# Attention tiles at the other end of SBUF, closed early; w_sp's norms, scale and block sums planned into the first stage's z2; plain units removed

## The chip, the cores and the metric

The kernel runs on one core of one Trainium2 chip. A core has five engines that run their own instruction streams: PE (TensorE, matrix products into eight PSUM banks of 128 x 512 f32), DVE (VectorE), ACT (ScalarE), POOL (GpSimd) and SP (SyncE, which here only issues DMAs). SBUF is the on-chip memory of 128 partitions. The metric is the device time of one execution in microseconds (us). Before the change three runs gave 1127.93, 1130.12 and 1130.16 us; the median is 1130.12 us.

## What is computed

Two layers, each an attention block and a gated MLP block, on x of 2048 x 576, in bfloat16. The attention looks at 8 positions at distance 2 and has 32 heads of 18. The MLP block mixes along the sequence with the 2048 x 2048 matrix w_sp:

```python
def _B_ref(x, w_in, w_sp, b_sp, w_out):
    z = _gelu(jnp.einsum('bsd,df->bsf', x, w_in))
    z1 = z[..., :Fh].copy()
    z2 = _layernorm(z[..., Fh:], axis=-1)
    g = jnp.einsum('ts,bsf->btf', w_sp, z2) + b_sp[None, :, None]
    return jnp.einsum('bsf,fd->bsd', z1 * g, w_out)

x = x + _A_ref(_layernorm(x, axis=-1), A_wqkv, A_wo)
x = x + _B_ref(_layernorm(x, axis=-1), B_w_in, B_w_sp, B_b_sp, B_w_out)
x = x + _A_ref(_layernorm(x, axis=-1), A_wqkv, A_wo)
x = x + _B_ref(_layernorm(x, axis=-1), B_w_in, B_w_sp, B_b_sp, B_w_out)
```

Both layers use the same weights. Fh is 2304.

## The kernel before

Five stages run one after the other: phase_F(0), phase_S(1), phase_F(2), phase_S(3), phase_E.

**phase_F** is an attention stage with z2 at its end. It describes its work as steps (name, engine, estimated cost, key, function, steps that must come before, buffers taken) and hands them to a planner, the class Flow. The planner simulates the engines with the estimated costs. It repeatedly takes the engine that can start something earliest, and on it, of the steps that can start at that time, the one with the lowest key (line 191). The order in which it takes the steps is the order in which instructions are issued, so each engine's stream is fixed when the kernel is built. A step that takes "H" needs a pair of PSUM banks, one that takes "PT" a single bank. The attention steps carry keys near the number of their tile (0 to 17), z2's steps the key KZ + KS * i with KZ = 169.61 and KS = 25.3 in the first layer (line 1056), for i from 0 to 15.

z2 of row tile i (Z2_steps, line 883) is three products of 128 x 768 on PE (lines 895 and 902), a gelu on ACT for each (918), a sum of squares on DVE (928) and ACT (933), eight small steps on POOL (939 to 946) and the normalisation on DVE (949). From i = 7 the products go in groups of three.

**phase_S** is the spatial stage. w_sp's rows are handled in two halves c of 1024, the upper half c = 0 first, and z in nine column blocks jj. Each (c, jj) is a unit, 18 in all, in an order written out by hand, with no planner. An ordinary unit (unit, line 1197) multiplies a 2 x 2 split of w_sp's half by z with seven block products for two column halves s: blocks A11, A12, S1, S2, S4, S3, A22, each 8 matmuls of 128 x 512 (eight, line 1181), 56 in all. S1 to S4 are sums and differences of the blocks in f16; T1 to T4 are the same kind of sums of z (t_op, line 1187), made on DVE one unit ahead. Between them stand plus (line 1205) and times_u (1195) on DVE. Each unit also makes z1 of the next one on PE (1156, 1164) with gelus on ACT (1168). The f16 blocks need w_sp multiplied by a power of two, which comes from the sum of all absolute values: norm_part (1077) sums one 128 x 2048 part on ACT or DVE, norm_sum (1085) adds up, scales (1088) totals over the partitions with a PE matmul against ones and makes scale and inverse in five small DVE steps.

In the first layer w_sp is not ready in blocks. So phase_S(1) loads the upper half with four transposing DMAs (line 1279, on SP) into A11, A12, S3's and A22's space, takes norms, and runs units 0 and 1 as plain units (line 1249): four blocks by two halves s, 64 matmuls each, on unscaled blocks in unit 0 and 1, while ACT and DVE take the norms of both halves and scale (lines 1329 to 1339) and DVE makes S1, S2, S4 and, in unit 2, S3 (1333, 1342, 1343, 1432). The lower half is made block by block in eight pieces during units 3 to 7: four transposing DMAs (piece_load), a scaling on ACT (1376), six sums on DVE (1383) and a store to DRAM on POOL's queue; the store of piece k starts the load of piece k + 2 on SP. The table at line 1350 says where in which unit each step of a piece stands. The finished blocks of the upper half are stored from line 1415 for the second layer, and unit 8 loads the lower half's blocks. phase_S(3) loads all from DRAM.

**Memory.** The tiles of phase_F, attention and others, come from one pool that closes when the phase ends. A tile of a later pool that lies over an earlier tile waits for the last use of that tile.

Of the kernel before, what the change touches and what calls it, by code (L numbers as in the profile page):

```python
# [10 lines left out]
ACT = mybir.ActivationFunctionType  # L11
# [9 lines left out]
P = 128  # L21
# [24 lines left out]
EPS = 1e-5  # L46
BLOCKS = ("A11", "A12", "A22", "S3", "S1", "S2", "S4")
# [219 lines left out]
class K:  # L267
# [17 lines left out]
    def setup(self):  # L285
# [23 lines left out]
        self.first_pairs = None  # L309
# [219 lines left out]
    def phase_F(self, li):  # L529
# [3 lines left out]
        pool = self.pool = cm.__enter__()  # L533
        x_prev = self.A_x if first else self.xres[0]
# [7 lines left out]
                  0.8 if first else 0.0, first)  # L542
        wB = pool.tile([P, 3, 2 * D], bf16, name="wB")
        zst = pool.tile([P, NS // 2, 11], f32, name="zst")
        Pb = [pool.tile([P, 4, 8, HP], bf16, name=f"P{k}") for k in range(2)]
        wo = pool.tile([P, 5, D], bf16, name="wo")
        vbi = [pool.tile([P, H * (DH + 1)], i32, name=f"v_ext{k}") for k in range(3)]
# [3 lines left out]
        oT = pool.tile([P, 5, RING], bf16, name="oT")  # L551
        o_tb = [pool.tile([P, D if first else D + HP], bf16, name=f"o_t{k}") for k in range(2)]
        oq = [self.zu[:, NB, a:a + 5 * P].rearrange("p (c n) -> p c n", n=P) for a in (0, 2176)]
        xt = {}

        def x_tile(i):
            if i < NXZ:
                return self.zu[:, NB - 1, D * i:D * (i + 1)]
            if i not in xt:
                xt[i] = pool.tile([P, D], bf16, name="xt", bufs=NX)  # L560
            return xt[i][:]
# [11 lines left out]
        QKb = [pool.tile([P, 16 * R], bf16, name=f"QK{k}") for k in range(NQK[ly])]  # L573
# [83 lines left out]
        def QK_steps(g, key):  # L657
# [16 lines left out]
            for d in range(NM):  # L674
# [6 lines left out]
                def ev(e, d=d):  # L681
                    if d % 2 == 0:
                        box["s", d // 2] = pool.tile([P, 4 * QT * max(sizes)], bf16, name="stg", bufs=NSTG[ly])
                    to = box["s", d // 2][:, 2 * gw * (d % 2):2 * gw * (d % 2 + 1)]
                    self.copy(e, to.rearrange("p (r q j) -> p q r j", q=2, r=2), box[d][:, :, 0:gw].rearrange("p q (j r) -> p q r j", r=2))
# [19 lines left out]
            def ev4(e):  # L705
                to = box[NM, "s"] = pool.tile([HP, 2 * QT * max(sizes)], bf16, name="stx", bufs=NSTX[ly])
# [51 lines left out]
        def ATT_steps(t, key):  # L758
# [42 lines left out]
            def fin(_):  # L801
                o_t = box["o"] = o_tb[t % 2][:, 0:D]
                O = box["O"][:, :, 0:16 * (DH + 1)].rearrange("p s (h e) -> p s h e", e=DH + 1)
                rec = pool.tile([P, 2, 16], f32, name="rec", bufs=2)
# [279 lines left out]

    def norm_sum(self, norms):
        self.nc.vector.tensor_reduce(out=self.wsc[:, 4:5], in_=norms, axis=AX.X, op=ALU.add)

    def scales(self, c, ones, ps):
# [3 lines left out]
        col = [wsc[:, k:k + 1] for k in range(7)]  # L1092
        bits = [k.bitcast(i32) for k in col]
        nc.tensor.matmul(ps, lhsT=ones, rhs=col[4], start=True, stop=True)
        self.pairs += 1
        nc.vector.tensor_copy(out=col[5], in_=ps)
# [5 lines left out]
    def phase_S(self, li):  # L1102
# [6 lines left out]
        low = ("S1",) if first else ("A22", "S1")  # L1109
        A = {n: pool.tile([P, 8, 512], f16 if n[0] == "S" else bf16, name=n) for n in low}  # L1110
        T = pool.tile([P, 4, 8, P], f16, name="T")
        tmp = [pool.tile([P, 512], f32, name=f"g{k}") for k in range(3)]
        A |= {n: pool.tile([P, 8, 512], f16 if n[0] == "S" else bf16, name=n) for n in ("S2", "S3", "S4", "A22", "A12", "A11") if n not in low}
# [12 lines left out]
        w1s = {}  # L1126

        def load_w1(jj, c):
            w1 = pool.tile([P, 2 * NM + 1, P], bf16, name="w1", bufs=2)
            self.load576(lambda s: w1[:, NM * s:NM * s + NM, :], w1[:, 2 * NM, :], self.B_w_in[:, P * jj:P * (jj + 1)],  # L1130
                         self.B_w_in[:, 1152 + P * jj:1152 + P * (jj + 1)], (nc.sync,))
            w1s[jj, c] = w1
# [54 lines left out]
        def t_op(jj, k):  # L1187

            B = z_of(jj)
            a, b = {1: (B[0, 1], B[0, 0]), 2: (B[1, 1], T[:, 0]), 3: (B[1, 1], B[0, 1]), 4: (B[1, 0], T[:, 1])}[k]  # L1190
            nc.vector.tensor_tensor(out=T[:, k - 1], in0=a, in1=b, op=ALU.subtract)
# [5 lines left out]
        def unit(n, jj, c, z1, t_next, at):  # L1197
# [21 lines left out]
            eight(v, T[:, 0], A["S1"], True)  # L1219
# [4 lines left out]
            eight(y, T[:, 1], A["S2"], False)  # L1224
# [7 lines left out]
            eight(y, T[:, 2], A["S3"], False)  # L1232
# [7 lines left out]
            eight(y, T[:, 3], A["A22"], False)  # L1240
# [8 lines left out]
        def plain(jj, c, banks, raw, order, after):  # L1249
            B, u = z_of(jj), u_of(jj, c)  # L1250
            met = set()
            for a, b in order:
                for s in range(2):
                    eight(self.psum[:, banks[a].start + s, :], B[b, s], raw[a, b], a not in met)
                after(a, b)
                if a in met:
                    for s in range(2):
                        g = tmp[(2 * a + s) % 3][:].bitcast(bf16)[:, 0:512]
                        nc.vector.tensor_tensor(out=g, in0=self.psum[:, banks[a].start + s, :], in1=bias(c, a), op=ALU.add)
                        times_u(u, a, s, g)  # L1260
                met.add(a)

        def load_ops(c, names):
            for nm in names:
                if c == 0:
                    self.dma(A[nm][:].rearrange("p i t -> p (i t)"), self.ops[c, nm][:])
                else:
                    to = A[nm][:].bitcast(bf16) if nm[0] == "S" else A[nm][:]
                    self.dma(to.rearrange("p i t -> p (i t)"), self.ops1[:, BLOCKS.index(nm), :])

        ORDER = ("A11", "A12", "S1", "S2", "S4", "S3", "A22")
        Wt = self.B_w_sp
        wAf = self.wA[:].rearrange("p a n -> p (a n)")
        todo = {}
        if first:
            raw = {(0, 0): A["A11"][:], (0, 1): A["A12"][:], (1, 0): A["S3"][:].bitcast(bf16), (1, 1): A["A22"][:]}
            for a in range(2):
                for b in range(2):
                    nc.sync.dma_start_transpose(out=raw[a, b], in_=Wt[512 * a:512 * a + 512, 1024 * b:1024 * b + 1024])
            load_w1(0, 0)  # L1280
            flat = {n: A[n][:].bitcast(bf16).rearrange("p i t -> p (i t)") for n in ("S1", "S2", "S4")}
            nat = [flat[n][:, 2048 * k:2048 * k + 2048] for n, k in (("S4", 0), ("S2", 0), ("S2", 1), ("S1", 0), ("S1", 1))]
            nat += [wAf[:, 2048 * k:2048 * k + 2048] for k in range(3)]

            def load_nat(k):
                self.dma(nat[k], Wt[1024 + P * k:1024 + P * k + P, :])
            for k in range(3):
                load_nat(k)
            load_w1(1, 0)
            for k in range(3, 7):  # L1290
                load_nat(k)
        else:
            load_ops(0, ("A11", "A12"))
            load_w1(0, 0)
            load_ops(0, ("S1", "S2", "S4", "S3"))
            load_w1(1, 0)
        q = nc.gpsimd if first else nc.sync
        load_b(0, 0, q)
# [230 lines left out]
```

## Time and profile before

| what | value |
|---|---|
| median of three runs | 1130.12 us |
| lowest and highest | 1127.93 and 1130.16 us |
| the profiled execution | 1131.26 us |
| its span, first to last instruction | 1129.5 us |
| mean granted TensorE clock | 0.997 |

A row of busy time by stretches gives start and end in us from the span's start, the length, then the busy us and the instruction count of each engine, the TensorE clock that was granted as a share of full speed, the busy share of the DMA engines and GB/s. A row of a timeline gives start, duration, engine, line of the kernel, operation, out<-in tiles and the number of instructions merged; in brackets stands how long the engine was idle before it and what ended that idle time. Matmuls overlap in their records, so steady progress is read from start to start. Rows of one line's instructions give min/median/max duration in ns.

### The profile page before, as it was taken

To read this page: it belongs to the slowest core of one execution; us is meant where nothing else is said; L and a number is where in the kernel's file an instruction comes from. 1 tells how busy PE (TensorE), PEld (TensorE's weight loads), DVE (VectorE), ACT (ScalarE), POOL (GpSimd) and SP (SyncE) were. 2 spreads that over 40 slices of the span, in tenths; PEclk is the share of its full clock that TensorE was granted. 3 is DMA by queue.
4 is the path that set the end of the run, shared out by engine and by line. 5 is a ranking of instruction groups with operands and counts; after the bars stand their busy time and mean duration, and the time that the engine had idled before them with its cause. 6 is when DMAs were issued, how large, how long until landed. Compare 5 with 4: busy or idle time off the path is not lost.

```text
span 1129.5 us, 24544 instructions
## 1 busy us (share of the span) xinstructions
PE 1108.1 (98%) x10163; PEld 614.6 (54%) x10163; DVE 696.5 (62%) x1152; ACT 442.1 (39%) x689; POOL 265.2 (23%) x574
## 2 busy tenths in 40 slices
PE   8899999999999999999999989999999999999998
PEld 5677655444434444447677765554444444444677
DVE  8788855687666555554566778556555555555311
ACT  7678877883232011102455678872101110111000
POOL 6244488501111000004101215882000000000000
PEclk9899999999999999999999999999999999999999
DMA  7776372345879532115344585702112283221221
GB/s 191 150 133 143 68 164 81 97 147 149 267 214 325 184 104 58 48 50 138 66 77 84 108 169 105 271 1 77 41 47 59 77 315 87 75 58 38 84 64 53
DMA packets 187304, 131.82 MB, mean 117 GB/s; under 512 B 145241, under 2 KB 171481, under 8 KB 183609
## 3 DMA queue, kind: packets, MB, share of 16 engines
q1 hardware_dynamic: 179864, 100.47, 35.0%
q0 software_dynamic: 7328, 29.79, 8.1%
q8 instruction: 79, 1.29, 0.5%
q14 instruction: 33, 0.26, 0.1%
HBM read 68.40 MB, written 31.20 MB: 88 GB/s over the span
## 4 chain that ended last, share of the span: by engine, by line
PE 65%; DVE 1%; ACT 1%; DMA 1%; issue 1%; POOL 0%; DVEq 0%; ACTq 0%; POOLq 0%
PE psum L1183 29%; PE psum L479 12%; PE psum L1156 8%; PE psum L895 6%; PE psum L389 3%; PE psum L737 2%; PE psum L863 1%; DMA S<-op 1%; PE psum L1164 1%; PE psum L902 1%; PE psum L797 1%; PE psum L775 1%; PE psum L383 0%; ACT P L782 0%; ACT v_ext L460 0%
## 5 line engine op out<-in xcount | busy, mean ns | idle before, releaser
L1168 ACT ACTIVATE zu<-psum 128x1024 bf16<-128x1024 f32 x72 | 73.2, 1022 | 396.8 <-PE psum L1164 363.8
L1205 DVE SCALAR_TENSOR_TENSOR g<-psum,wsc,bsp 128x512 f32<-128x512 f32 (+1 forms) x136 | 101.9, 750 | 141.7 <-PE psum L1183 141.5
L1183 PE MATMUL psum<-S,T 128*128 128x512 f16 x816 | 187.2, 379 | 1.0 <-DVE g L1205 0.9
L1183 PEld LDWEIGHTS <-T 128*128 128x128 f16 x1088 | 106.3, 98 | 130.0 <-issue 1.9
L1183 PEld LDWEIGHTS <-zu 128*128 128x128 bf16 x944 | 92.4, 98 | 114.7 <-issue 3.8
L1183 PE MATMUL psum<-A,zu 128*128 128x512 bf16 x640 | 144.2, 379 | 0.0
L1156 PE MATMUL psum<-xnD,w 128*128 128x512 bf16 x576 | 136.3, 380 | 0.0
L479 PEld LDWEIGHTS <-zu 128*128 128x128 bf16 x1152 | 112.3, 98 | 29.6 <-issue 0.4
L1205 DVE SCALAR_TENSOR_TENSOR g<-psum,wsc,g 128x512 bf16<-128x512 f32 x102 | 76.5, 750 | 57.3 <-PE psum L1183 56.8
L895 PE MATMUL psum<-wA,xnD 128*128 128x384 bf16 x576 | 109.7, 327 | 0.4 <-DVE v_ext L459 0.2
L479 PE MATMUL psum<-wA,zu 128*128 128x288 bf16 x768 | 105.4, 286 | 0.2 <-DVE v_ext L459 0.2
L895 PEld LDWEIGHTS <-xnD 128*128 128x128 bf16 x768 | 72.1, 98 | 56.1 <-issue 11.9
L1156 PEld LDWEIGHTS <-w 128*128 128x128 bf16 x576 | 53.4, 98 | 74.6 <-issue 15.3
L918 ACT ACTIVATE zu<-psum 128x768 bf16<-128x768 f32 x96 | 77.0, 805 | 27.2 <-PE psum L902 17.6
L928 DVE CUSTOM_DVE_ANT_1 zu<-zu 128x1536 bf16<-128x1536 bf16 x32 | 56.2, 1757 | 43.9 <-ACT zu L918 43.8
L1183 PE MATMUL psum<-S,zu 128*128 128x512 f16 (+1 forms) x304 | 71.5, 379 | 3.3 <-DVE g L1205 3.3
L782 ACT ACTIVATE P<-psum 128x912 bf16<-128x912 f32 x72 | 64.3, 944 | 11.9 <-PE psum L775 10.1
L389 PE MATMUL psum<-xnD,wqk 128*128 128x228 bf16 (+1 forms) x480 | 66.2, 285 | 2.1 <-ACT xnD L460 1.2
L1195 DVE TENSOR_TENSOR zu<-g,zu 128x512 bf16<-128x512 bf16 x144 | 61.2, 425 | 9.1
L1183 PE MATMUL psum<-A,T 128*128 128x512 bf16 x272 | 64.2, 379 | 0.0
L283 POOL DMA_DIRECT2D ustore<-zu x18 | 12.8, 708 | 188.9 <-ACT zu L1168 120.9
L389 PEld LDWEIGHTS <-wqk 128*128 128x128 bf16 x480 | 44.5, 99 | 17.4 <-issue 7.9
(140 smaller groups left out, 1414.8 us busy)
## 6 DMA issues: line engine op xcount, KB each, us to landing
w<-in_B_w_in_dram SPq DMA_DIRECT2D x72, 128.0 KB
ustore<-zu POOLq DMA_DIRECT2D x18, 512.0 KB, 3.7
zu<-ustore SPq DMA_DIRECT2D x18, 512.0 KB
S<-op SPq DMA_DIRECT2D x8, 1024.0 KB
A<-op SPq DMA_DIRECT2D x6, 1024.0 KB
QK<-stg SPq DMA_DIRECT2D x36, 114.0 KB
QK<-stg SPq DMA_DIRECT2D x24, 171.0 KB
op_S<-S POOLq DMA_DIRECT2D x4, 1024.0 KB, 6.8
```

The lines of the kernel that those rows point to most:

```text
L389: nc.tensor.matmul(ps(s), lhsT=lhsT, rhs=rhs, start=(c == 0 and not rest_first), stop=(c == NM - 1 and rest_first))
L479: nc.tensor.matmul(ps[:, hh, 0:288], lhsT=u[:, s * S + i * P:s * S + (i + 1) * P], rhs=wout(b, s)[:, hh * 288:(hh + 1) * 288], start=(b == ...
L737: self.read_xn_strided(nc.tensor.matmul(ps[to, s, 0:288].rearrange("p (b n) -> p b n", b=2), lhsT=self.xnD[rows, c, c0 + s:c0 + P:2], rhs= ...
L782: nc.scalar.activation(out=Psb[:, 2 * hh:2 * hh + 2, :, 0:QH], in_=box["L", hh][:, :, 0:8 * QH].rearrange("p a (b c) -> p a b c", c=QH), f ...
L895: nc.tensor.matmul(box[u][:, s, 0:384], lhsT=self.xnD[:, c, at], rhs=(win2a[:, c, s] if c < NM - 1 else win2b[:, s])[:, cols], start=(firs ...
L918: nc.scalar.activation(out=self.zu[:, 3 * u:3 * u + 3, 256 * i:256 * (i + 1)].rearrange("p j (s r) -> p s j r", s=2), in_=box[u][:, :, 0:3 ...
L928: nc.vector.tensor_tensor_reduce(out=junk(0, 6), in0=z[:, 0:6, :], in1=z[:, 0:6, :], scale=1.0 / FH, scalar=0.0, op0=ALU.mult, op1=ALU.add ...
L1156: nc.tensor.matmul(ps[:, h, :], lhsT=w1[:, NM * h + d, :], rhs=self.xnD[:, d, t0:t0 + 512], start=(opens and d == 0), stop=(not opens and ...
L1168: nc.scalar.activation(out=u_of(jj, c)[:, :, 512 * k:512 * k + 512], in_=ps, func=ACT.Gelu_apprx_tanh)
L1183: nc.tensor.matmul(ps, lhsT=lhs[:, i, :], rhs=rhs[:, i, :], start=(opens and i == 0), stop=(i == 7), skip_group_check=not opens)
L1195: nc.vector.tensor_tensor(out=uv, in0=g, in1=uv, op=ALU.mult)
L1205: nc.vector.scalar_tensor_tensor(out=out, in0=ps, scalar=inv[c], in1=other, op0=ALU.mult, op1=ALU.add)
```

## The change

- A second pool "A" on the right side of SBUF takes the attention tiles of phase_F (P, wo, v_ext, oT, o_t, QK, stg, stx, rec). The step "blocks" closes it after the last attention products (w0.m1 to w15.m1) and opens there a pool "B" with the seven block tiles.
- In the first layer, make_ops adds steps to the planner with keys 901 to 919: four transposing loads (SP), eight norms (four ACT, four DVE), the sum "nrm" (DVE), the total "sc0.m" (PE, takes one bank), the scale "sc0" (DVE), four multiplications "times" and four sums "sum" (DVE). In the second layer, load_first_ops adds the seven block loads on SP.
- phase_S: units 0 and 1 are ordinary units; z1 of unit 0 and its four t_op come first. The lower half's norms run on ACT in units 0 and 1, from loads on POOL's queue. The pieces start in unit 2 and the stores of the upper half's blocks in unit 0. T is four tiles; w1's first load comes first; b_sp is loaded on SP.
- phase_E: the spacer tile "below" goes.

```diff
+        acm = tc.tile_pool(name=f"A{li}", bufs=1, side="right", reuse_waits="tile")
+        att = acm.__enter__()
...
-        Pb = [pool.tile([P, 4, 8, HP], bf16, name=f"P{k}") for k in range(2)]
-        wo = pool.tile([P, 5, D], bf16, name="wo")
+        Pb = [att.tile([P, 4, 8, HP], bf16, name=f"P{k}") for k in range(2)]
+        wo = att.tile([P, 5, D], bf16, name="wo")
...
+        fl.step("blocks", "SP", 0.0, 900, lambda _: self.open_blocks(li + 1, acm), [f"w{i}.m1" for i in range(NS)])
+        (self.make_ops if first else self.load_first_ops)(fl)
...
+    def open_blocks(self, li, acm):
+        acm.__exit__(None, None, None)
+        self.bcm = self.tc.tile_pool(name=f"B{li}", bufs=1, side="right", reuse_waits="tile")
+        pool = self.bcm.__enter__()
+        self.blk.update({n: pool.tile([P, 8, 512], f16 if n[0] == "S" else bf16, name=n) for n in PLACED})
...
+    def load_first_ops(self, fl):
+        for k, nm in enumerate(ORDER):
+            fl.step(f"op{nm}", "SP", 0.4, 901 + k, lambda _, nm=nm: self.load_ops(0, (nm,)), ["blocks"], lag=5.0)
...
+        for k, (a, b) in enumerate(four):
+            fl.step(f"raw{k}", "SP", 2.2, 901 + k, lambda _, a=a, b=b: load(a, b), ["blocks"], lag=7.0)
+        for k in range(8):
+            on = "DVE" if k % 2 else "ACT"
+            fl.step(f"nrm{k}", on, 2.25 if k % 2 else 2.1, 901 + k, lambda e, k=k: norm(e, k), [f"raw{k // 2}"])
+        fl.step("nrm", "DVE", 0.3, 910, whole, [f"nrm{k}" for k in range(8)])
+        fl.step("sc0.m", "PE", 0.1, 910, total, ["nrm"], takes=[("PT", "sc0.ps")], mode="w", pairs=1)
+        fl.step("sc0", "DVE", 0.75, 910, lambda _: self.scales(0, box["ps"]), ["sc0.m"], ["sc0.ps"])
+        for k, (a, b) in enumerate(four):
+            fl.step(f"times{k}", "DVE", 1.3, 911 + k, lambda _, a=a, b=b: times(a, b), ["sc0"])
+        raw = self.raw
+        for k, (nm, x, y, op, pre) in enumerate((
+                ("S1", lambda: raw(1, 0), lambda: raw(1, 1), ALU.add, ["times2", "times3"]),
+                ("S2", lambda: A["S1"][:], lambda: raw(0, 0), ALU.subtract, ["sum0", "times0"]),
+                ("S4", lambda: raw(0, 1), lambda: A["S2"][:], ALU.subtract, ["sum1", "times1"]),
+                ("S3", lambda: raw(0, 0), lambda: raw(1, 0), ALU.subtract, ["sum0"]))):
+            fl.step(f"sum{k}", "DVE", 2.3, 916 + k,
+                    lambda _, nm=nm, x=x, y=y, op=op: nc.vector.tensor_tensor(out=A[nm][:], in0=x(), in1=y(), op=op), pre)
...
+        z1_a(0, 0, pr[0:2])
+        z1_b(0, 0, pr[0:2])
+        for k in (1, 2, 3, 4):
+            t_op(0, k)
...
+            def load_nat(k):
+                self.dma(nat[k], Wt[1024 + P * k:1024 + P * k + P, :], nc.gpsimd)
...
+            def first_sums(n, where):
+                k = {(0, "A11"): 0, (0, "A12"): 1, (0, "S1"): 2, (0, "S2"): 3, (0, "S4"): 4, (0, "S3"): 5,
+                     (1, "A11"): 6, (1, "A12"): 7}.get((n, where))
+                if k is not None:
+                    self.norm_part("ACT", nat[k], norms[:, k:k + 1], nat[k])
+                    if k + 3 < 8:
+                        load_nat(k + 3)
...
-                    ((3, "begin"), (3, "S1"), (3, "S2")), ((3, "S3"), (3, "A22"), (3, "end")),
-                    ((4, "S1"), (4, "S3"), (4, "second")), ((4, "A22"), (5, "A12"), (5, "S1")),
-                    ((5, "S3"), (5, "A22"), (5, "end")), ((6, "A12"), (6, "S2"), (6, "S4")),
-                    ((6, "A22"), (7, "A12"), (7, "S1")), ((7, "S2"), (7, "S3"), (7, "second")))):
+                    ((2, "A11"), (2, "S1"), (2, "S2")), ((2, "second"), (2, "end"), (3, "A11")),
+                    ((3, "S2"), (3, "S3"), (3, "second")), ((4, "A11"), (4, "S1"), (4, "S2")),
+                    ((4, "second"), (4, "end"), (5, "A11")), ((5, "S4"), (5, "second"), (5, "A22")),
+                    ((6, "A12"), (6, "S2"), (6, "S4")), ((7, "begin"), (7, "A12"), (7, "S1")))):
...
-            if first and n < 2:
-                continue
```

In the table of pieces each entry names the unit and the place of the scaling, of the first sums, and of the last sums with the store.

More of the change, by code (lines that the diff above doesn't have):

```diff
@@ L1275, in phase_S @@
-        if first:
[L1276 to L1283, printed above, removed]
+        load_b(0, 0, nc.sync)
```

221 lines of the change are left out of this document (88 added, 133 removed).

## The prediction, made before the changed kernel was run

> **What bounds the kernel now.** I read first the busy table of the page, then busy time by stretches, then TensorE's timeline where the changed stretch begins and ends, and last the other engines there.
>
> ```profile
> span 1129.5 us, 24544 instructions
> PE 1108.1 (98%) x10163; PEld 614.6 (54%) x10163; DVE 696.5 (62%) x1152; ACT 442.1 (39%) x689; POOL 265.2 (23%) x574
> ```
>
> TensorE works 98% of the span. So a change gains only by giving it less to do or by closing one of its few gaps, and it loses whatever gap it opens.
>
> ```profile
> core 0: us, PE busy (x) PEld busy (x) DVE busy (x) ACT busy (x) POOL busy (x), PEclk, DMA share, GB/s
> 142.00:160.00 18.00, 18.00 (x117) 9.09 (x115) 10.53 (x12) 15.24 (x36) 15.48 (x34) 1.00 0.60 123
> 160.00:207.00 47.00, 47.00 (x307) 25.18 (x305) 27.44 (x31) 35.41 (x81) 41.29 (x86) 1.00 0.41 100
> 207.00:264.44 57.44, 56.59 (x271) 25.03 (x270) 46.12 (x61) 41.13 (x38) 8.51 (x17) 1.00 0.48 140
> 264.44:280.62 16.18, 16.18 (x78) 7.06 (x76) 12.05 (x24) 5.83 (x4) 2.19 (x3) 1.00 0.54 181
> ```
>
> The first two rows are the first stage's z2, the third the start of the spatial stage (two plain units and the first ordinary one), the fourth one ordinary unit. During z2 TensorE has no idle time at all, VectorE (DVE) is idle 47.00 - 27.44 = 19.56 us of its main part and ScalarE (ACT) 11.59 us.
>
> ```profile
> 205.16 0.66 PE L902 MATMUL psum<-wB,xnD 64*128 64x384 bf16 x6
> ...
> 207.07 1.89 PE L1156 MATMUL psum<-xnD,w 128*128 128x512 bf16 x8
> ...
> 215.26 3.62 PE L1183 MATMUL psum<-A,zu 128*128 128x512 bf16 x16
> 218.72 3.62 PE L1183 MATMUL psum<-S,zu 128*128 128x512 bf16 x16
> ...
> 256.77 1.89 PE L1183 MATMUL psum<-S,T 128*128 128x512 f16 x8 [0.85 <-DVE g L1205]
> ...
> 264.44 3.62 PE L1183 MATMUL psum<-A,zu 128*128 128x512 bf16 x16
> ...
> 339.47 1.89 PE L1183 MATMUL psum<-S,zu 128*128 128x512 f16 x8 [3.07 <-DVE g L1205]
> ```
>
> z2 ends at 207.07, when z1 of units 0 and 1 begins; the first plain unit begins at 215.26, unit 3 at 264.44. The last row is the largest gap of the stage, in unit 7.
>
> **Plain units removed.** Before, z2's end to unit 3 takes 264.44 - 207.07 = 57.37 us. After, it is z1 of unit 0 alone, half of 215.26 - 207.07, or 4.10 us, and three ordinary units of 16.18 us: 52.64 us. That is -4.73 us if nothing waits; the 0.85 us gap is in it.
>
> **Pieces.** The blocks of the second half of w_sp are made in pieces between units.
>
> ```profile
> 333.99 2.00 ACT L1376 ACTIVATE wA<-wA,wsc 128x2048 bf16<-128x2048 bf16 x1 [14.27 <-DMA wA<-in_B_w_sp_dram]
> ```
>
> Piece 6 landed late, its sums stood in DVE's order ahead of the unit's own work, and TensorE lost the 3.07 us. Its load starts behind the store of piece 4. In before's table those sums come 1 unit and 3.5 us behind that store; in the new one the store stands at A11 of unit 5 and the sums at S2 of unit 6, 16.18 us and three block products (5.2 us) apart, 1.7 us more, and the whole chain runs a unit earlier. I take -3.1 us; bounds 0 (another piece is as late) and -3.1.
>
> **Loads and norms moved into z2.** Closing the attention pool lets the four transposed loads of w_sp start when the last attention product is done, on SP ahead of the last y transposes.
>
> ```profile
> 137.66 1.40 PE L863 MATMUL psum<-wo,oT 128*128 128x288 bf16 x10
> ```
> ```profile
> 150.94 8.99 SPq L1279 DMA_TRANSPOSE A<-in_B_w_sp_dram  x2
> 159.99 4.25 SPq L1279 DMA_TRANSPOSE S<-in_B_w_sp_dram  x1
> 164.28 3.97 SPq L1279 DMA_TRANSPOSE A<-in_B_w_sp_dram  x1
> ```
>
> From about 139.5 at the same pace of 17.3 us, with two y transposes between, all are issued by about 159. y14 and y15 then land up to 9 us later, and z14 and z15 ask for them only after 190: no cost. The norms are four on each engine:
>
> ```profile
> L1081 ACT ACTIVATE wA<-A x3: 1902/1910/1911, 216.4 to 222.5; 128x2048 bf16<-128x2048 bf16 x3
> L1083 DVE TENSOR_REDUCE wA<-A x3: 2269/2278/2279, 213.1 to 219.7; 128x1 f32<-128x2048 bf16 x3
> 205.60 0.81 ACT L918 ACTIVATE zu<-psum 128x768 bf16<-128x768 f32 x1 [1.00 <-POOL zst L940]
> ```
>
> DVE: 4 x 2.28 = 9.1 us into 19.56 us idle, and no PSUM bank waits for DVE in z2: nothing. ACT: 4 x 2.1 (with the accumulator's read) = 8.4 us into 11.59, one gap of 1.0 us to each z2 group of 4.6. A norm put into such a gap holds the next gelu up by 1.1 us. TensorE opens a group every 4.6 us and has four bank pairs; it asks for the pair of a group's first product again 5.9 us after opening it (4.6 and one product of 1.3), and its gelu ends at about 4.1, so TensorE bears some 1.8 us. But the planner counts 0.83 us for a gelu and 0.87 for the square where the trace needs about 0.93 and 1.03, so it packs norms closer than ACT can follow. I take +1.0 us, bounds 0 and +2.5.
>
> **Scale, products and sums: where I expect the loss.** "sc0.m", TensorE's product that totals the norms, has key 910; z2's steps have 169.61 + 25.3 i, at most 549. The planner gives a free engine the lowest key among the steps that can start. A z2 step needs a bank pair and sc0.m one bank, but in z2 banks come free by pairs, so whenever sc0.m could start, a z2 step can too. As TensorE never idles in z2, sc0.m is chosen behind z2's last matmul, about 207.1, though its norms were ready some 25 us before. What hangs on it is all on DVE: five small scale steps, four multiplications "times", four sums. Each engine works in its order of issue, and the spatial stage's first DVE work (T1) is issued behind them.
>
> ```profile
> 207.33 1.76 DVE L928 CUSTOM_DVE_ANT_1 zu<-zu 128x1536 bf16<-128x1536 bf16 x1 [1.73 <-ACT zu L918]
> ...
> 209.26 0.94 DVE L949 TENSOR_SCALAR zu<-zu,zst 128x2304 bf16<-128x2304 bf16 x1 [0.16 <-POOL zst L946]
> 212.28 0.95 DVE L949 TENSOR_SCALAR zu<-zu,zst 128x2304 bf16<-128x2304 bf16 x1 [2.07 <-POOL zst L946]
> ...
> 230.35 0.15 DVE L1096 COPY wsc<-psum 128x1 f32<-128x1 f32 x1
> ...
> 231.04 0.68 DVE L1191 TENSOR_TENSOR T<-zu 128x1024 f16<-128x1024 bf16 x1
> ...
> 236.32 1.29 DVE L1332 TENSOR_SCALAR A<-A,wsc 128x4096 bf16<-128x4096 bf16 x1 [0.47 <-PE psum L1183]
> 237.70 2.29 DVE L1333 TENSOR_TENSOR S<-S,A 128x4096 f16<-128x4096 bf16 x1
> 239.91 0.68 DVE L1259 TENSOR_TENSOR g<-psum,bsp 128x512 bf16<-128x512 f32 x1
> ```
>
> From z2's end DVE has z15's square (1.84 with its read), two normalisations (1.88), the scale (231.04 - 230.35 = 0.69), four products (5.16) and four sums at 2.21 (239.91 - 237.70; 8.84): 18.41 us. Begun at 207.35, behind the total's matmul, they end at 225.8, and T1 (0.68) at 226.4. TensorE wants T1 for the product with S1. Without a wait that comes 4.10 + 16 matmuls (218.72 - 215.26 = 3.46) behind 207.07, at 214.6. So it is 11.8 us late: **+11.8 us**; bounds +10.8 (products overlapping as the sums do) and +13.1. Before, this work was hidden under the plain units' 64 matmuls each and partly on ACT (two of the multiplications); that cover is what is removed. POOL runs z15's small chain meanwhile:
>
> ```profile
> 207.38 1.84 POOL L946 TENSOR_SCALAR zst<-zst 128x1 f32<-128x1 f32 x1
> ...
> 211.97 0.27 POOL L946 TENSOR_SCALAR zst<-zst 128x1 f32<-128x1 f32 x1
> ```
>
> The same step lasts 1.84 us while L928 runs on DVE and 0.27 when DVE is idle. A z15 normalisation that is late for this stalls DVE, up to 1.3 us: the upper bound above. The Trainium skill ("SBUF — State Buffer", section "Who interferes with whom") has GpSimd fully blocked for the length of a VectorE instruction that holds the port pair they share; the two rows agree.
>
> **Restart.** TensorE then stands idle from about 217 to 226.
>
> ```profile
> 45.60:48.60 3.00, 0.03 (x2) 0.01 (x1) 0.82 (x2) 1.20 (x2) 0.00 (x0) 0.94 1.22 101
> 48.60:55.90 7.30, 7.30 (x73) 5.25 (x73) 3.55 (x6) 1.44 (x3) 0.54 (x1) 0.56 0.40 91
> 336.40:339.47 3.07, 0.00 (x1) 0.00 (x1) 2.95 (x8) 1.42 (x2) 0.18 (x1) 1.00 0.39 88
> ```
>
> After 3.0 us of idling TensorE had a granted clock of 0.56 for 7.3 us; after the 3.07 us in unit 7 it kept 1.00. Nine idle microseconds are nearer the first: 7.3 x (1 - 0.56) = 3.2 us lost. Without a slow clock, the second S product would wait some 0.9 us for g0 behind T2 to T4; at the slow clock that is hidden. I take +3.2, bounds +0.9 and +3.7 (7.3 at a half).
>
> The Trainium skill ("TensorE: Matmul & The Clock Gate", section "What's actually happening") says the clock halves after an idle window of about 3.4 us and returns after about 3.4 us of work. By it the restart would cost 1.7 us of lost work; row 48.60:55.90 shows a return twice as long, and I keep the row.
>
> **The rest at nothing.** Eight norms of the lower rows move to units 0 and 1 on ACT: 8 x 2.1 = 16.8 us in 32 us, where an ordinary unit without pieces has two gelus; without that cover a late gelu would hold DVE's products, up to 2 us. Their loads go to POOL's queue behind z15's chain. In the second layer seven loads of ready blocks move ahead of the last y transposes on SP; z2 there leaves tens of microseconds. The last stage's weights get other space, released one product later.
>
> **Sum.** The profiled execution took 1131.26 us (1129.5 of span and 1.76 around it): 1131.26 - 4.73 - 3.1 + 1.0 + 11.8 + 3.2 = 1139.4. The median of the runs is 1.14 lower than the profiled time, so **1138.3 us**. Its own range: low ends 1131.26 - 4.73 - 3.1 + 0 + 10.8 + 0.9 - 1.14 = 1134.0; high ends -4.73 - 0 + 2.5 + 13.1 + 3.7 give 1144.7.
>
> **Rivals.** (1) The tail is hidden: sc0.m finds a place inside z2. For it: DVE's idle 19.56 us there, and some more before 160, nearly hold the 23 us of norms, products and sums. Against it: the keys, and TensorE without one gap. Then the 11.8 and 3.2 fall to about 1 us of leftover: 1131.26 - 4.73 - 3.1 + 1.0 + 1.0 - 1.14 = 1124.3, faster. It decides whether the total's matmul runs before about 190. (2) ACT becomes z2's bound and none of its 8.4 us hides: 7.4 more than forecast, 1145.7. Against it: 11.59 us idle. (3) The change does not do what it says: the loads still wait for z2's end. Then 17.3 us of loads, a norm, the scale, products and sums follow 207, T1 comes near 242, 27 us late, 15.6 more than forecast: about 1154. Against it: before's loads already began at 150.94, inside z2.
>
> **Numbers.** Forecast 0.73, rival 1 0.17, rival 2 0.05, rival 3 0.02, 0.03 for halves between. A measurement here tells 0.2% (2.3 us) from no change. Faster 0.19, same 0.02, slower 0.79. As both signs hold much, the range reaches rival 1's value and rival 2's: 1124 to 1146; the forecast's own is 1134 to 1144.7.
>
> **What would show it.** Right: the total's matmul directly behind z2's last; times and sums solid on DVE for about 18 us behind it; a TensorE gap near 9 us before the first product with S1, released by DVE's T1; a slow clock after it; no gap in unit 7; units still 16.18 us. Wrong: sums on DVE before 200; S1's product starting near 215; ACT gaps filled and TensorE idle inside z2.

## The result, and the profile after

The median of four runs after the change is 1141.35 us (1140.89 to 1147.88); before, 1130.07 us over four runs of the same session. The ratio is 1.0118 (95% interval 1.008 to 1.0156): slower, at the place forecast, and by 11.3 us where 8.2 were forecast (1138.3 against 1130.12). The profiled execution took 1141.22 us, its span 1139.5, 10.0 us longer than before's.

TensorE's timeline of the changed kernel behind z2's end comes first. Before, TensorE had no gap from there up to 256.77 us.

```profile
202.97 0.28 PE L1165 MATMUL psum<-wsc,S 128*128 128x1 f32 x2
203.11 1.89 PE L1231 MATMUL psum<-xnD,w 128*128 128x512 bf16 x7
...
208.75 3.40 PE L1258 MATMUL psum<-A,zu 128*128 128x512 bf16 x15 [1.38 <-DVE A L1141]
214.59 0.39 PE L1258 MATMUL psum<-A,zu 128*128 128x512 bf16 x1 [2.44 <-DVE zu L952]
218.57 3.57 PE L1258 MATMUL psum<-S,T 128*128 128x512 f16 x8 [3.60 <-DVE S L1159]
227.65 3.54 PE L1258 MATMUL psum<-S,T 128*128 128x512 f16 x8 [5.50 <-DVE g L1280]
```

The total's matmul (L1165) stands directly behind z2's last. Then come four gaps, 12.92 us together, all released by VectorE: a multiplied block, z15's normalisation, the sum S1, and the first plus. VectorE's timeline shows what lies ahead of each.

```profile
207.42 3.66 DVE L1141 TENSOR_SCALAR A<-A,wsc 128x4096 bf16<-128x4096 bf16 x3
213.59 0.94 DVE L952 TENSOR_SCALAR zu<-zu,zst 128x2304 bf16<-128x2304 bf16 x1 [2.50 <-POOL zst L949]
214.45 1.27 DVE L1141 TENSOR_SCALAR S<-S,wsc 128x4096 bf16<-128x4096 bf16 x1
215.63 0.69 DVE L1266 TENSOR_TENSOR T<-zu 128x1024 f16<-128x1024 bf16 x1
216.24 2.29 DVE L1159 TENSOR_TENSOR S<-S,A 128x4096 f16<-128x4096 bf16 x1
218.44 0.69 DVE L1266 TENSOR_TENSOR T<-zu,T 128x1024 f16<-128x1024 bf16 x1
219.04 2.29 DVE L1159 TENSOR_TENSOR S<-S,A 128x4096 f16<-128x4096 f16 x1
221.24 0.69 DVE L1266 TENSOR_TENSOR T<-zu 128x1024 f16<-128x1024 bf16 x1
221.84 4.49 DVE L1159 TENSOR_TENSOR S<-A,S 128x4096 f16<-128x4096 bf16 x2
226.25 0.69 DVE L1266 TENSOR_TENSOR T<-zu,T 128x1024 f16<-128x1024 bf16 x1
226.85 0.75 DVE L1280 SCALAR_TENSOR_TENSOR g<-psum,wsc,bsp 128x512 f32<-128x512 f32 x1
```

The sums stand between T1 and T4, not all ahead of T1. So TensorE waits twice, once for S1 itself and once for the first plus behind T4. Busy time by stretches gives what z2 looked like to each engine, and the granted clock:

```profile
160.00:203.00 43.00, 43.00 (x282) 22.99 (x280) 26.87 (x33) 36.95 (x82) 38.00 (x76) 1.00 0.02 7
203.00:272.81 69.81, 56.67 (x249) 23.86 (x252) 50.51 (x78) 28.62 (x31) 17.13 (x31) 0.90 0.55 168
...
216.00:218.00 2.00, 0.00 (x0) 0.10 (x1) 2.00 (x2) 2.00 (x3) 0.56 (x1) 0.84 0.43 168
218.00:230.00 12.00, 5.92 (x14) 1.97 (x14) 11.71 (x12) 6.54 (x8) 2.15 (x4) 0.50 0.78 251
230.00:232.00 2.00, 2.00 (x8) 0.79 (x7) 1.18 (x3) 0.00 (x0) 0.00 (x0) 0.74 0.17 70
```

The ACT norms cost z2 nothing (TensorE is busy for all 43.00 us). The last three rows are the low clock: it falls within the third gap and returns behind the fourth.

Where the 10.0 us come from, by stretches between landmarks on TensorE (first z1 matmul; unit 3's start; start of the second attention stage; first z1 matmul of the second layer):

| stretch | before | after | difference | foreseen |
|---|---|---|---|---|
| start to z2's end | 207.07 | 203.11 | -3.96 | +1.0 |
| z2's end to unit 3 | 57.37 | 69.70 | +12.33 | +10.27 |
| unit 3 to second attention | 240.67 | 237.44 | -3.23 | -3.1 |
| second attention and z2 | 258.85 | 263.30 | +4.45 | 0 |
| the rest | 365.5 | 365.95 | +0.4 | 0 |

The second row's 69.70 us are 4.10 of z1, three units of 16.18, 12.92 of gaps, and 4.1 that are left. Of these about 3.5 are the low clock, by the last two rows above: TensorE is busy 5.92 us at 0.50 and 2.00 us at 0.74, which loses 5.92 x 0.50 + 2.00 x 0.26 = 3.48 us. The other 0.6 are read from no row. The first and the fourth row were not foreseen and nearly cancel; experiments 3 and 4 ask about them.

### The profile page after: what moved, and what is told of

It is laid out like the page before. It is cut to its first block, busy times and chain, and to the rows that moved or that the text cites. A ratio compares the mean times of both kernels' runs of the same rounds, so it can differ in the third digit from the quotient of the medians.

```text
span 1139.5 us, 24503 instructions
## 1 busy us (share of the span) xinstructions
PE 1107.1 (97%) x10109; PEld 613.8 (54%) x10147; DVE 709.2 (62%) x1173; ACT 431.4 (38%) x684; POOL 271.7 (24%) x580
## 5 line engine op out<-in xcount | busy, mean ns | idle before, releaser
L1258 PE MATMUL psum<-S,T 128*128 128x512 f16 x864 | 201.7, 384 | 9.1 <-DVE g L1280 5.5
L1280 DVE SCALAR_TENSOR_TENSOR g<-psum,wsc,bsp 128x512 f32<-128x512 f32 (+1 forms) x144 | 108.0, 750 | 155.4 <-PE psum L1258 155.1
L1258 PEld LDWEIGHTS <-T 128*128 128x128 f16 x1152 | 113.4, 98 | 147.8 <-issue 12.4
L1258 PEld LDWEIGHTS <-zu 128*128 128x128 bf16 x864 | 84.7, 98 | 106.9 <-DVE zu L952 2.9
L1258 PE MATMUL psum<-A,zu 128*128 128x512 bf16 x576 | 130.4, 379 | 3.8 <-DVE zu L952 2.4
L481 PEld LDWEIGHTS <-zu 128*128 128x128 bf16 x1152 | 112.5, 98 | 30.7 <-issue 1.6
L1280 DVE SCALAR_TENSOR_TENSOR g<-psum,wsc,g 128x512 bf16<-128x512 f32 x108 | 81.0, 750 | 62.8 <-PE psum L1258 62.5
L898 PEld LDWEIGHTS <-xnD 128*128 128x128 bf16 x768 | 72.4, 98 | 57.1 <-issue 13.3
L1258 PE MATMUL psum<-A,T 128*128 128x512 bf16 x286 | 67.9, 379 | 0.5 <-DVE g L1280 0.4
L1258 PE MATMUL psum<-S,zu 128*128 128x512 f16 x288 | 68.0, 379 | 0.2 <-DVE g L1280 0.2
```

The costliest lines, as they stand in the source:

```text
L481: nc.tensor.matmul(ps[:, hh, 0:288], lhsT=u[:, s * S + i * P:s * S + (i + 1) * P], rhs=wout(b, s)[:, hh * 288:(hh + 1) * 288], start=(b == ...
L898: nc.tensor.matmul(box[u][:, s, 0:384], lhsT=self.xnD[:, c, at], rhs=(win2a[:, c, s] if c < NM - 1 else win2b[:, s])[:, cols], start=(firs ...
L1258: nc.tensor.matmul(ps, lhsT=lhs[:, i, :], rhs=rhs[:, i, :], start=(opens and i == 0), stop=(i == 7), skip_group_check=not opens)
L1280: nc.vector.scalar_tensor_tensor(out=out, in0=ps, scalar=inv[c], in1=other, op0=ALU.mult, op1=ALU.add)
```

## The experiments

Each was timed against the kernel before on the same chip (median there 1128.5 to 1128.7 us, and 1130.07 for the first row). "Gaps" is TensorE's idle time of 0.3 us or more from z2's end to the second attention stage, "stretch" that whole stretch (before 298.04, after 307.14).

| run | median us | ratio to before, 95% | stretch | gaps |
|---|---|---|---|---|
| after | 1141.35 | 1.0118 (1.0080 to 1.0156) | 307.14 | 13.3 |
| e1: total early | 1139.12 | 1.0095 (1.0065 to 1.0125) | 304.92 | 12.4 |
| e2: total, products, sums early | 1141.69 | 1.0120 (1.0084 to 1.0155) | 307.78 | 13.6 |
| e9: pairs on POOL | 1140.70 | 1.0113 (1.0099 to 1.0127) | 305.70 | 11.0 |
| e6: e1 with pairs | 1131.32 | 1.0022 (1.0005 to 1.0038) | 298.86 | 5.2 |
| e5: e2 with pairs | 1130.59 | 1.0021 (1.0009 to 1.0033) | 297.17 | 4.1 |
| e11: e6 with loads on SP | 1131.61 | 1.0030 (1.0018 to 1.0043) | 297.21 | 4.9 |
| e10: e5 with loads on SP | 1130.39 | 1.0012 (0.9999 to 1.0025) | 296.90 | 3.6 |
| e12: e10 with z1 of unit 1 first | 1127.45 | 1.0003 (0.9987 to 1.0018) | 292.56 | 2.2 |
| e8: after, loads on SP | 1143.15 | 1.0122 (1.0097 to 1.0147) | 305.75 | 12.1 |
| e4: after, second layer's loads late | 1141.34 | 1.0107 (1.0077 to 1.0136) | 306.51 | 12.9 |
| e3: before, tiles at the other end | 1129.26 | 1.0003 (0.9986 to 1.0020) | 300.01 | 4.3 |
| e7: before, pairs on POOL | 1127.21 | 0.9986 (0.9974 to 0.9998) | 296.77 | 2.6 |

**1 and 2. Is it the place of the total?** The prediction said that the place of sc0.m decides. Two runs move it.

```diff
-        fl.step("sc0.m", "PE", 0.1, 910, total, ...
-        fl.step("sc0", "DVE", 0.75, 910, ...
+        fl.step("sc0.m", "PE", 0.1, -50, total, ...
+        fl.step("sc0", "DVE", 0.75, -50, ...
```

> The changed kernel with one thing moved: the total's matmul (sc0.m) and the scale's five small VectorE instructions take their place in z2 right behind the sum of the norms (171.8 us in the changed kernel's trace) instead of behind z2's last matmul (202.97 us). The four multiplications and four sums keep their places among the z2 steps (behind them by key). Theory (the place of the total holds 20 us of VectorE work back until z2 is over): part of the four multiplications and four sums now lies inside z2, the gaps of TensorE between z2's end and unit 3 (1.38 + 2.44 + 3.60 + 5.50 = 12.9 us, and the 0.50 clock behind them) shrink to less than half, and the time falls by 4 to 14 us from 1141.3 to 1127 to 1137 us. Rival (VectorE has no room in z2 for that work: the stall only moves, into z2, or to the norms' chain of z15): within 2 us of 1141.3 us, with new TensorE gaps inside z2 or the 2.44 us gap at z15 grown.

The second run also gives the multiplications and sums keys of -40 and -30 and up.

> As the run before it, and the four multiplications and four sums also take their place as soon as the scale is there, ahead of the z2 steps that are ready then. Theory: all of the 20 us of VectorE work lies inside z2, no TensorE gap at the first spatial units is released by it, and what is left is the gap that z15's norm makes (2.44 us or less): 1124 to 1129 us, the time of my rival 'tail hidden' (1124.3) and faster than the kernel before (1130.1). Rival 1 (no room on VectorE): 20 us of VectorE in one piece hold up z2's own normalisations, z2's steps on POOL and ScalarE pile up behind them and the stall comes at z15's norm: more than 1133 us. Rival 2 (the stall is z15's chain on POOL, not VectorE): the 2.44 us gap stays and the time is 1130 us or more.

The total ran at 172.34 us (e1) and 171.42 us (e2), 31 us earlier than in the changed kernel. e1's median is 2.2 us lower, where theory had 4 to 14, and its interval overlaps that of the changed kernel. e2 won nothing and stands 12.7 us above its forecast of 1124 to 1129: the theory fell. Both rivals named for e2, VectorE without room and the chain on POOL, fit its time; the runs with pairs, below, tell them apart. TensorE's timeline of e2:

```profile
212.03 0.39 PE L1258 MATMUL psum<-A,zu 128*128 128x512 bf16 x1 [2.28 <-DVE zu L952]
215.03 0.61 PE L1258 MATMUL psum<-A,zu 128*128 128x512 bf16 x1 [2.62 <-DVE zu L952]
218.04 0.61 PE L1258 MATMUL psum<-A,zu 128*128 128x512 bf16 x1 [2.40 <-DVE zu L952]
221.06 0.61 PE L1258 MATMUL psum<-A,zu 128*128 128x512 bf16 x1 [2.41 <-DVE zu L952]
225.52 0.61 PE L1258 MATMUL psum<-A,zu 128*128 128x512 bf16 x1 [3.85 <-DVE zu L952]
```

All waits are now for normalisations of z. A product over all tokens needs every row tile of z, and the last came at 224.51 us instead of 213.59. VectorE was idle 2.1 us or more ahead of each of the last of them, waiting for POOL. POOL's timeline of e2, first beside VectorE's solid work, then the catching up (the first of eight instructions of each row tile):

```profile
172.85 1.17 POOL L949 TENSOR_SCALAR zst<-zst 128x1 f32<-128x1 f32 x1
174.10 1.04 POOL L942 TENSOR_TENSOR zst<-zst 128x1 f32<-128x1 f32 x1
189.33 1.80 POOL L943 TENSOR_TENSOR zst<-zst 128x1 f32<-128x1 f32 x1 [14.19 <-DVE zst L931]
...
211.07 0.19 POOL L942 TENSOR_TENSOR zst<-zst 128x1 f32<-128x1 f32 x1
214.08 0.19 POOL L942 TENSOR_TENSOR zst<-zst 128x1 f32<-128x1 f32 x1
217.09 0.19 POOL L942 TENSOR_TENSOR zst<-zst 128x1 f32<-128x1 f32 x1
```

While VectorE made 14 us of products and sums in one piece, its squares were late, and POOL had nothing to do for 14.19 us. It then worked without a break, but one row tile takes it 4.39 us beside a square (206.68 to 211.07) and 3.01 us (214.08 to 217.09) even where VectorE has only a normalisation to do, and TensorE delivers one every 4.6 us; the lost 14 us were not made up by z2's end. In e1, with the work spread between the squares, POOL was held inside its own instructions instead:

```profile
172.16 0.27 POOL L945 TENSOR_SCALAR zst<-zst 128x1 f32<-128x1 f32 x1
176.47 2.75 POOL L945 TENSOR_SCALAR zst<-zst 128x1 f32<-128x1 f32 x1
193.65 3.76 POOL L945 TENSOR_SCALAR zst<-zst 128x1 f32<-128x1 f32 x1
```

The same 128x1 instruction takes 0.27 us alone, 2.75 beside a square and a multiplication, 3.76 beside a sum and a square. It ends where VectorE's pair ends (197.41 us; the square runs from 195.61 to 197.36).

**5, 6, 7 and 9. Take POOL's load away.** The small statistics of two row tiles are made at once, nine instructions of 128x2 instead of sixteen of 128x1, in the first layer only.

```diff
+            def small2(_):
+                j = i % (NS // 2)
+                c = [zst[:, j - 1:j + 1, k] for k in range(11)]
...
+            elif i % 2:
+                fl.step(tag + ".p", "POOL", 4.6, key, small2, [f"z{k}.{x}" for k in (i - 1, i) for x in "qr"])
+                for t, f in norms[-2:]:
+                    fl.step(t + ".n", "DVE", 0.94, key, f, [tag + ".p"])
```

> The run with all of the total, multiplications and sums early in z2, with one thing more: the first layer's small statistics on POOL (eight instructions of 128x1 for each z2 step, some 4.3 us) are made for two z2 steps at once, nine instructions of 128x2 for each pair; only the first layer's z2 is changed. Theory P (what holds the first spatial units up is POOL: it is busy 8.8 of 10 us in z2, stands still while a long VectorE instruction runs, and has no slack for 14 us of them, so z15's normalisation slides from 209 to 225 us): with half of POOL's instructions z15's normalisation is done by about 212, TensorE's gaps between z2's end and unit 3 (13.6 us in that run) fall below 4 us, and the time is 1121 to 1128 us. Rival V (VectorE itself has no room): the gaps stay above 9 us and the time at 1137 to 1142.

> The same pairs on POOL, with only the total's matmul and the scale placed early, multiplications and sums where the planner's keys put them between the z2 steps. Theory P: 1121 to 1129 us, gaps below 5 us (12.4 in the run without pairs), POOL's 128x1 and 128x2 instructions no longer end after 212 us. Rival V: 1135 to 1140.

> A control: the kernel before, with the same pairs on POOL and nothing else. TensorE has no gap in z2 there and z15's normalisation (213 us) is in time for the first plain unit (215 us), so by theory P and by rival V alike the pairs gain nothing: 1127 to 1130 us, within 0.2% of before. If it is faster by more than 0.3%, the pairs help by themselves and the two runs above must be read against this one.

> The fourth corner of the square: the changed kernel with POOL's statistics made in pairs and nothing else; the total's matmul stays behind z2's last matmul, and so do multiplications and sums. The other corners are 1141.4 us (neither), 1141.7 (early alone) and 1130.6 (both). If the two hindrances are in series (VectorE's tail by its place, POOL by its load, each enough to hold the first units up), pairs alone bring little too: 1138 to 1141.5 us, with the gaps that wait for a sum and for g0 still there (9 us in the changed kernel). If pairs alone do all of it, and the place of the total never mattered: 1129 to 1132.

Pairs with everything early took 11.1 us off e2 (1141.69 to 1130.59), and pairs with the total early 7.8 us off e1 (1139.12 to 1131.32). The mechanism is as theory P has it; the size is short of its 1121 to 1128 for e5 and 1121 to 1129 for e6. The last normalisation came at 213.61 us, 1.6 us later than P named, and one gap was left, with a low clock behind it. Busy time of e5 over the main part of z2, and two timelines of it:

```profile
160.00:203.00 43.00, 43.00 (x282) 23.29 (x281) 37.78 (x40) 35.45 (x78) 29.73 (x35) 1.00 0.02 5
```
```profile
174.79 2.27 POOL L962 TENSOR_TENSOR zst<-zst 128x2 f32<-128x2 f32 x1
177.14 2.26 POOL L963 TENSOR_SCALAR zst<-zst 128x2 f32<-128x2 f32 x1
...
202.60 0.20 POOL L962 TENSOR_TENSOR zst<-zst 128x2 f32<-128x2 f32 x1
202.88 0.22 POOL L963 TENSOR_SCALAR zst<-zst 128x2 f32<-128x2 f32 x1
```
```profile
214.61 0.61 PE L1278 MATMUL psum<-A,zu 128*128 128x512 bf16 x1 [4.05 <-DVE zu L966]
```

VectorE is now busy 37.78 of 43 us and TensorE still never waits in z2: the room on VectorE was there, and rival V falls. The two halves of the second fence show the hold again: beside sums of 2.3 us each, POOL gets one small instruction in per sum; alone each takes 0.2 us.

The square of four is complete: neither 1141.35, early alone 1141.69, pairs alone 1140.70, both 1130.59. Pairs alone still wait 5.47 us for the first plus at 225.16 us, the tail of the changed kernel. Either hindrance alone holds the first units up for as long. The control, the kernel before with pairs, is at 0.9986 of before: by itself this edit is worth 0 to 0.3%.

**8, 10 and 11. The lower rows' loads on POOL's queue.** Three of them stand inside the last statistics.

```diff
-                self.dma(nat[k], Wt[1024 + P * k:1024 + P * k + P, :], nc.gpsimd)
+                self.dma(nat[k], Wt[1024 + P * k:1024 + P * k + P, :], nc.sync)
```

> The changed kernel with one thing moved: the loads of the lower rows for their norms (eight, 0.55 to 0.74 us of POOL each to issue) go from POOL's queue to SP's, so that the first three no longer stand between z14's and z15's small chains on POOL. Theory N (they make z15 late, the 2.44 us gap at 214.59 us): that gap shrinks to below 1 us, but the sums behind it on VectorE then set the start, so the time falls by 0 to 2.4 us: 1139 to 1141.5. Rival P': z15's chain is late because VectorE's multiplications hold POOL up, not for the loads: the gap stays above 1.5 us and the time at 1141.

> Early total, multiplications and sums, POOL's statistics in pairs, and the lower rows' loads on SP's queue instead of POOL's. In the run without the last edit three of these loads (2.0 us of POOL between 208.6 and 211.4 us) stand in the last pair's chain, which ends at 213.55 us, and TensorE waits 4.05 us and then runs at a clock of 0.53 to 0.78. Theory: the chain ends 2 us earlier, the gap falls to 2 us, the time by 2 us to 1128.5; if the shorter gap also spares the low clock, by 4 to 5 us to 1125 to 1127, below the kernel before. Rival (POOL's chain then waits for something else, or SP's queue delays the weights of the next units): 1130 or more.

> The same with only the total and the scale early, multiplications and sums spread between z2's steps: 3.6 us of gap in the run without the last edit. Theory: 1127 to 1129.5 us, and 1125 to 1127 if the low clock is spared. Rival: 1131 or more.

In e8 z15's gap fell from 2.44 to 1.63 us, above the 1.5 that rival P' named: without the loads POOL was held 2.30 us by the multiplications. Theory N fell. The time did not fall (1143.15 us, nothing to be told from 1141.35). In e10 the gap fell to 3.01 us, the time by 0.2, inside the noise: the store of a block took the place of one load on POOL, and the low clock stayed, 0.71 over the 10 us behind the gap. In e11 nothing was gained either. Both theories missed; the times are those that their rivals named.

**12. Cover for what is left.** z1 of unit 1 moves from between unit 0's products to ahead of them.

```diff
         z1_b(0, 0, pr[0:2])
+        if first:
+            z1_a(1, 0, pr[0:2])
+            z1_b(1, 0, pr[0:2])
...
-            z1 = nxt
+            z1 = None if first and n == 0 else nxt
```

> The run with early total, multiplications and sums, POOL's statistics in pairs and the loads on SP's queue, with one thing moved: z1 of unit 1 (4.1 us of TensorE) stands behind z1 of unit 0, ahead of unit 0's products, instead of between unit 0's last products. No work is added. In the run without it TensorE has done unit 0's z1 and 14 of 16 first products 3.0 us before z15's normalisation, and then 10 us follow at a clock of 0.66. Theory: the 4.1 us fill that wait, the gap falls below 0.5 us, and with it the low clock behind it; 3.0 us of gap and 10 x (1 - 0.66) = 3.4 us of clock come back: 1124 to 1127 us, below the kernel before by 2 to 4 us. Rival (the low clock comes anyway, or the wait moves to T1, the first plus or unit 1's gelu): 1128 us or more.

TensorE's timeline of e12:

```profile
206.71 1.89 PE L1251 MATMUL psum<-xnD,w 128*128 128x512 bf16 x8 [0.63 <-ACT zu L1263]
...
210.80 3.62 PE L1278 MATMUL psum<-A,zu 128*128 128x512 bf16 x15
214.25 1.89 PE L1278 MATMUL psum<-S,T 128*128 128x512 f16 x8
216.54 1.89 PE L1278 MATMUL psum<-S,T 128*128 128x512 f16 x8 [0.40 <-DVE g L1300]
```

In this execution the wait for z15 is gone, and with it the low clock; small waits of 0.3 to 0.8 us took its place. The stretch takes 292.56 us, 5.5 less than before, so of the 4.73 and 3.1 us that the prediction expected from plain units and pieces most is won here at last. But the profiled execution took 1125.26 us and is the fastest of twelve, which reach up to 1133.68. The median is 1127.45, between theory's 1127 and the rival's 1128, and the ratio to before (0.9987 to 1.0018) tells no difference; nor does it from e10, whose interval overlaps, so the gain over e10 is shown in the stretch and not in the time. Against the changed kernel e12 wins 14 us. Part of what the stretch should win against before is lost in the second attention stage, which takes 262.77 us here, 1.1 to 3.9 more than in the three profiles with plain units.

**3. The first attention stage.** The kernel before, with the attention tiles in a pool on the right side and nothing else:

```diff
+        acm = tc.tile_pool(name=f"A{li}", bufs=1, side="right", reuse_waits="tile")
+        att = acm.__enter__()
```

> The kernel before, with only the attention tiles placed in a pool at SBUF's other end (closed at the same point as the other pool, so no load starts earlier), plain units kept. It asks where the 4.1 us come from that the changed kernel gained before z2's end (207.07 to 202.97 us, with the 2.97 us idle of TensorE at 45.6 us and the 0.56 clock of 7.3 us behind it gone). Theory A (placement alone): the idle at 45.6 us is gone or below 1 us here too, the first z1 matmul comes at about 203 us, and the time is 1126 us. Theory B (something else, such as the order of the steps that the planner writes out, or the first layer's code): the idle at 45 us and the low clock stay and the time is 1130 us, within 0.2%.

The idle time at 45 us was absent and z2 ended at 201.70 us, as theory A said; the time was 1129.26, as theory B said. Of the 5.4 us that z2 ended earlier, 4.4 came back: the stretch is 1.97 us longer than before's and the second attention stage 2.40, and both have a low clock in this execution. The kernel before with pairs (e7) had no idle time at 45 us either (z2's end at 201.67), and e8, a variant of the changed kernel, had it (2.83 us, end at 205.85). So the -3.96 us of the first row belong to the one execution that was profiled before, not to the change. In e3 the low clock stood behind this gap:

```profile
334.19 2.76 PE L1186 MATMUL psum<-S,zu 128*128 128x512 f16 x8 [2.34 <-DVE g L1208]
```
```profile
334.19:336.00 1.81, 1.81 (x7) 0.77 (x7) 1.81 (x3) 0.31 (x1) 1.33 (x2) 0.74 0.89 179
336.00:338.00 2.00, 2.00 (x6) 0.63 (x5) 0.98 (x2) 1.69 (x1) 0.00 (x0) 0.50 1.02 327
```

**4. The second attention stage.** The changed kernel with the second layer's block loads back at the start of its spatial stage.

```diff
-        (self.make_ops if first else self.load_first_ops)(fl)
+        if first:
+            self.make_ops(fl)
...
+        if not first:
+            self.load_ops(0, ORDER)
```

> The changed kernel with the second layer's seven block loads moved back out of z2 to the start of the second spatial stage; the first layer is untouched. It asks where the 4.45 us come from that the second attention stage and z2 lost (258.85 to 263.30 us). Theory A (the planner's order with seven more SP steps in it, or the loads' traffic): that stage falls back to about 259 us; the second spatial stage may then wait for its blocks (up to some 10 us at its start). Theory B (other placement of the tiles, or a chance clock drop): the stage stays at 262 to 264 us, and the time changes only by what the late loads cost.

The stage took 264.88 us: theory A falls, the loads are not the cause. Over all profiles it takes 258.85, 261.25 and 261.69 us in the three kernels with plain units and 262.5 to 265.0 in the eleven without. Part of the difference is one transfer. SyncE's queue before and after:

```profile
500.12 0.91 SPq L283 DMA_DIRECT2D wB<-in_B_w_out_dram x2
```
```profile
510.44 0.91 SPq L285 DMA_DIRECT2D wB<-in_B_w_out_dram  x2
```

The stage starts at 505.11 and 510.25 us. The weights' load goes out 5 us ahead of it before, 0.2 us behind it after, and TensorE waits 0.18 and 0.85 us for them. In e3, whose pools lie like the changed kernel's but with wB in its old order, it goes out 5 us ahead.

The larger part is the clock. In the changed kernel TensorE has 6.83 us at a granted clock of 0.50 in this stage (688.42 to 695.24), and in before's profiled execution none. But e3 and e7, which keep the plain units, have 6.83 us at 0.50 there too (from 676.39 and 673.51); TensorE is idle in the stage for nearly as long as before (4.78 and 5.02 us against 4.70), and it takes 2.40 and 2.84 us longer. The second layer of e7 is before's own code. So about 2.4 of the 4.45 us need no change of the kernel. The idle time of the changed kernel is 6.33 us, 1.63 more than before. Besides the wait for the weights, waits of 0.68 us for v_ext and 0.73 for o_t stand in all eleven profiles without plain units and in none of the three with them, so they belong to the change; e4 shows that the loads do not cause them, and what does stays open.

## Why the prediction came out right, and where it was wrong

- **Plain units, -4.73, and the pieces, -3.1.** Right. Units 1 and 2 take 16.3 and 16.18 us; there is no gap in unit 7, and the stretch behind unit 3 is 3.23 us shorter. But that gap is 3.07, 2.34 and 1.07 us in the three profiles with the old pieces (before, e3, e7), so -3.1 is the size of one execution.
- **ACT norms in z2, +1.0.** Nothing: TensorE was busy 43.00 of 43.00 us. No gelu held a bank up for as long as I had feared.
- **The tail, +11.8.** Its place was right: the total directly behind z2's last matmul, products and sums behind it. It measured 12.92 us, inside the bounds. The waits behind 215 us make 9.10 of it, near the 9 us of the forecast, but in two pieces, released by the sum S1 and by the first plus. That T1 stands behind all sums was wrong: the sums and the hand-written stage's T1 to T4 stand interleaved on VectorE, T1 came at 215.63, and S1 and the first plus were late in its place. A wait of 2.44 us for z15 was named as an upper bound (1.3 us) and was larger, for the loads on POOL's queue and the multiplications held it up.
- **Restart, +3.2.** About 3.5 us by the rows of the low clock, inside the bounds. It was not one restart: the clock stayed low through the last wait.
- **First and second attention stage.** Taken as unchanged; -3.96 and +4.45 us in the profiled pair. The first is chance. Of the second about 2.4 us are a low clock that kernels with plain units show as well, and 1.63 are idle time that goes with the change. The two rows nearly cancel, so the sum's closeness (1138.3 against 1141.35) owes something to luck.
- **Rival 1, the step that failed.** "DVE's idle 19.56 us there, and some more before 160, nearly hold the 23 us of norms, products and sums", and "It decides whether the total's matmul runs before about 190". In e1 and e2 it ran at 172 and 171 us, and they won 2.2 us and nothing. The room on VectorE exists (e5 uses it), but the chain from square to normalisation passes through POOL, which before's own row shows busy 41.29 of 47.00 us. I had read the row for ACT and DVE and not for POOL, although the prediction quoted POOL's 1.84 us against 0.27. What decides is POOL's load together with the total's place; and with both hindrances gone, e5's 1130.59 us still stand 6 us above rival 1's 1124.3.

The Trainium skill ("SBUF — State Buffer", section "Who interferes with whom") has VectorE's instructions with two SBUF inputs contend with GpSimd's reads, and in its two-port modes the one that comes second to the shared port pair fully blocked for the whole instruction. The rows of e1 and e5 agree, for the sums (2.27 us against 0.20) as for square and multiplication (2.75 against 0.27).

## What to carry to other kernels

An engine's idle time is room only if the chain that feeds and drains it has room too: before moving work into idle VectorE time, read the busy share of every engine that its neighbours' steps pass through, and whether those slow down beside it. Two hindrances, each long enough by itself, hide one another, so undoing either alone shows nothing; only the square of both settles it. A small last wait can be easier to cover with work that is due anyway than to shorten: here three runs that shortened it won nothing, and covering it took 4.3 us off the stretch of the profiled execution (296.90 to 292.56).

## What was not expected of the hardware

- The clock's fall does not go by the gap's length alone: 0.50 behind 2.34 us of idle time (e3, unit 7), 1.00 behind 3.07 us at the same place before. The Trainium skill ("TensorE: Matmul & The Clock Gate", section "What's actually happening") has a free-running window of about 3.4 us. The traces agree: every low stretch inside the fourteen profiles lasts 3.41 us or a multiple of it (3.41, 6.83, 13.65, 17.07). In e3 all of the 2.34 us lie in the 3.41 us that end where the clock falls (331.65 to 335.06). In before, counted on in steps of 3.41 from the clock's return at 55.09, a border at 338.39 splits the 3.07 us into 2.00 and 1.07. So a window need not be idle throughout, and where it starts matters. How much idle time it takes is not settled: in e10 the clock fell behind a window with 1.93.
- Two DMA issues on POOL's queue took 2.52 us together beside VectorE's multiplications in the changed kernel, and again in e4, where its other issues take 0.54 to 0.94 each: issuing DMAs from POOL is held up too.
